# Thirteen first-layer units in seven products instead of nine, with a first product that ScalarE copies between PSUM banks, in an order given as a table

## The chip, the cores and the metric

The kernel runs on one core of one Trainium2 chip. The metric is the device time of one execution in microseconds (us). Before the change it is 273.97 us, the median of three runs (273.91 to 274.48).

## The reference

The input is q, k and v of 8 batch elements, 8 heads, 576 positions and head size 64, and four weight matrices. An attention with a window of 128 positions and a linear bias by distance feeds an MLP mixer: a token mix over the 576 positions and a channel mix of 512 to 1536 to 512 channels, each with a residual.

```python
scores = scale * np.matmul(q, k.transpose(0, 1, 3, 2))
scores = np.where(mask, scores + bias[None], -1000000000.0)     # 0 <= i - j < 128
attn = softmax(scores);  x = attn @ v                           # as (batch, 576, 512)
h = np.maximum(x.transpose(0, 2, 1) @ w_tok1, 0.0) @ w_tok2     # 576 -> 256 -> 576
u = x + h.transpose(0, 2, 1)
out = u + np.maximum(u @ w_ch1, 0.0) @ w_ch2                    # 512 -> 1536 -> 512
```

## The kernel before

The 576 positions of a batch element are four blocks of 128 and a tail of 64; the tails of two elements share a tile. Work goes in eight stages, `b` = 0 to 7, one for each element. In stage `b` TensorE (PE) does `main(b)`, the channel mix of element `b`, and between its pieces `side(b + 1)`, the attention and the token mix of the next element.

- `side`: the keys and queries of a block are turned (`qkT`, by SP's transposing DMAs from the eleventh block on), `scores` multiplies them, ScalarE (ACT) takes the exponential into `pe`, VectorE (DVE) multiplies by a mask, `values` multiplies by v, and DVE or ACT divide into `xb`. `token_mix` then does two products (`W1`, a ReLU into `r1`, `W2`); DVE adds the residual to the second one (L907) and writes `ub`, or `utl` for a tail. SP turns `ub` block by block into `uT` (L915, `utl` into `uTt`), which is the input of `main`.
- `main`, first layer: a *chunk* (L1085) is one of the twelve hidden tiles of 128: four matmuls of 128x512, and one ReLU by ACT or DVE into `r2`. A *unit* (`unit`, L1006) does four hidden tiles at once by seven products (Strassen's way) of four matmuls of 128x256 each, with sums of weights (`WS`) and of inputs (`tt`) that DVE prepares. `UNITS` says how many of the three possible units a stage has; the rest are chunks.
- `main`, second layer (`second`, L1326): always seven products, in three PSUM banks `g1`, `g2` and `g3`, with sums `s` of the hidden values. Each product is evicted by a DVE add into an output buffer (`raw` or `ob`), then stored.

PSUM has eight banks, all a tile `ps`. In a unit the banks are y, z and w. Product 1 is made in y and `keep` copies it to an output buffer e1 in SBUF (L1021 on ACT, L1022 on DVE); y goes on to take products 6, 7 and 4 on top. Product 2 is made in z, and `join` adds z and e1 on DVE into `r2` (L1030) and applies the ReLU in place (L1032 on DVE, L1034 on ACT).

The order of all instructions is made in Python while the program is built. `Plan.run` takes, for each of the five engines, the operation that can begin first by costs and ranks, chooses the buffer of each ring, and for operations with a second engine (`other`) the engine. POOL issues the loads in the order of the list `LOADS` and of the pairs after it. Each engine then runs its instructions strictly in that order and waits on semaphores. `Plan.emit` puts matmuls of zeros (L1418) into gaps that the plan sees on PE in the first 60 us, so that its clock stays up.

Of the kernel before, what the change touches and what calls it, by code (L numbers as in the profile page):

```python
# [10 lines left out]
ALU = mybir.AluOpType  # L11
# [8 lines left out]
class Buf:  # L20
    def __init__(self, ring, choice):
        self.ring, self.choice, self.slot = ring, choice, None
        self.writers, self.parts, self.users = [], {}, []
# [6 lines left out]
class Ring:  # L30
# [14 lines left out]
    def best(self, choice, skip=0):  # L45
        got = []
        for c in choice:
            ts = [self.free(i) for i in c]
            if None not in ts:
                got.append((max(ts), c))  # L50
        got.sort(key=lambda x: x[0])
        return got[skip] if len(got) > skip else None

    def take(self, b):
        b.slot = self.best(b.choice)[1]
        for i in b.slot:
            self.owner[i] = b
            self.log[i].append(b)
# [15 lines left out]
class Plan:  # L74
    def __init__(self):
        self.rings, self.ops, self.orders, self.part, self.inside = {}, [], 0, 0, {}
# [4 lines left out]
    def buf(self, name, choice=None):  # L81
        return Buf(self.rings[name], choice or self.rings[name].each)

    def op(self, eng, cost, emit, rank, makes=(), adds=(), part=None, uses=(), reads=(), needs=(),
# [8 lines left out]
        o.n = len(self.ops)  # L93
# [35 lines left out]
    def run(self):  # L129
        ops = self.ops  # L130
        for o in ops:
            o.rank += SHIFT * offset(o)
# [82 lines left out]
        while todo:  # L215
            best = None
            for e, c in cand.items():
                pick, early = None, None
                for o in c:
                    if e == "POOL" and o is not pool[sent]:  # L220
# [8 lines left out]
                    for b in o.bufs:  # L229
                        if b.slot is None:  # L230
                            got = b.ring.best(b.choice, asked.count(b.choice))
# [19 lines left out]
                if early and early[1] is not pick[1] and early[0][0] < pick[0][0] + GRACE * pick[1].cost:  # L251
# [13 lines left out]
            todo -= 1  # L265
            for b in o.bufs:
# [43 lines left out]
    def emit(self, spin):  # L310
        banks = self.rings["ps"]
        fills = []
        for a, z in self.gaps:
            if a < FILL and z - a > (250 if a > DENSE else 60):
                for i, log in enumerate(banks.log):
                    spans = [(min(u.t0 for u in b.users), max(u.done for u in b.users)) for b in log]
# [27 lines left out]
RELU = 350  # L344
SUMS_AT = 60e3
# [17 lines left out]
UNITS = [0,0,0,1,2,1,2,3]  # L363
# [22 lines left out]
def kernel(  # L386
# [51 lines left out]
    def bank(choice=ONE):  # L438
        return plan.buf("ps", choice)
# [106 lines left out]
    for i_, raw in enumerate(raws):  # L546
        buf, i = block(0, (0, RAW)[i_ // 2])["qk"], i_ % 2

        def cast(eng=dve_.tensor_copy, raw=raw, buf=buf, i=i):
# [3 lines left out]
                **({"other": ("ACT", 600, lambda cast=cast: cast(act_.copy))} if i_ > 1 else {}))  # L553
    if PADT:
        for i in range(2):
            plan.op("DVE", 190, lambda i=i: dve_.memset(W1p[(1 - i) * R : (2 - i) * R, i, :], 0.0), -90)
# [103 lines left out]
    def transposes(pr, blk, rank):  # L660
        got = held[pr, blk]["qk"]
# [35 lines left out]
    def scores(pr, blk, half, rank, behind=()):  # L697
        tail = blk == TAIL
# [5 lines left out]
        sp = [bank(TWO + THIRD + [(6, 7)])] if joint else [bank(TWO + THIRD if first else TWO) for _ in range(2)]  # L704
# [13 lines left out]
        def go():  # L718
            for i in range(4):
                for kind, kb, a, z in work:  # L720
                    for e in range(2):
                        pe_.matmul(wide(e)[:, i, 0 if joint else kind, a:z],  # L722
                                   lhsT=ts[kb]()[e * D : (e + 1) * D, NHP + i, :],
                                   rhs=ts[blk]()[e * D : (e + 1) * D, i, a:z], start=not slanted, stop=True,
                                   skip_group_check=slanted)
# [49 lines left out]
    def values(pr, blk, half, pb, rank):  # L775
        xb = xbs[pr]
# [54 lines left out]
    def token_mix(b, rank):  # L831
        pr, half = b // 2, b % 2
# [6 lines left out]
        t1 = [bank() for _ in range(NJ)]  # L839
# [12 lines left out]
        def tails():  # L852
            for j in range(NJ):
# [6 lines left out]
        plan.op("PE", 225 if xt else 432, tails, rank(216), adds=t1,  # L860
                reads=[(xb, (TAIL, k)) for k in ((0, 1) if pad and pr < HALVED else (tk,))],
                uses=[xt] if xt else [], needs=lw1 if b else lw1[:2], mode=0 if pad else 1)
# [9 lines left out]
        hts = []  # L872
        for blk in blocks:
            wide = b == 0
            if wide and blk < 2:
                hts.append(bank(TWO))
            ht = hts[blk % 2] if wide else bank()
# [3 lines left out]
            def go(blk=blk, ht=ht, hs=hs, fold=fold):  # L881
                for j in range(NJ):
# [4 lines left out]
                    else:  # L887
                        c = blk % NC
                        pe_.matmul(ht()[:, hs], lhsT=W2[:, j, c * P : (c + 1) * P], rhs=r1()[:, j, :],  # L889
                                   start=j == 0, stop=j == NJ - 1 and not fold)  # L890
# [563 lines left out]
```

## Time and profile before

| what | before |
|---|---|
| time, median of 3 runs | 273.97 us (273.91 to 274.48) |
| the profiled execution: its span, first to last instruction | 273.4 us |
| PE busy | 267.6 us, 98% of the span, 2839 matmuls |
| DVE busy | 230.4 us, 84% |
| ACT busy | 148.9 us, 54% |
| POOL busy | 112.9 us, 41% |
| granted TensorE clock, mean | 0.999 |

The profile has the span of its execution and not that execution's own device time; the median of the runs lies 0.6 us above the span, which is what lies around the instructions. Busy time counts a moment once, however many matmuls overlap in it. A matmul's recorded duration contains the way through the array, so what one costs the stream is read from the distance between starts.

### The profile page before, as it was taken

How to read it: one execution, taken by the hardware profiler on the slowest of the kernel's cores; microseconds unless marked ns; L12 is line 12 of the kernel's file. 1: busy time of each engine (PE TensorE's matmuls, PEld its weight loads, DVE VectorE, ACT ScalarE, POOL GpSimd, SP SyncE). 2: the span in 40 equal slices, each digit the busy share in tenths (PEclk: the TensorE clock that was granted, in tenths of full speed). 3: DMA queues.
4: the chain of work that ended last, by engine and by line, in shares of the span. 5: the costliest groups of instructions: out<-in, count | busy, mean ns of one | idle time of the engine just before them, and what ended most of it. 6: DMA issues, size and time to landing. Idle time of an engine off the chain costs nothing.

```text
span 273.4 us, 7106 instructions
## 1 busy us (share of the span) xinstructions
PE 267.6 (98%) x2839; PEld 190.0 (69%) x2839; DVE 230.4 (84%) x543; ACT 148.9 (54%) x258; POOL 112.9 (41%) x142
## 2 busy tenths in 40 slices
PE   8999999999999999989999999999999999999994
PEld 4675667575568556765778868586578676888884
DVE  6577799998989499855999979998898899968984
ACT  5384895356931683038951079615960596047720
POOL 8999645950770077500890007800940300040000
PEclk9999999999999999999999999999999999999999
DMA  8999999999998999999999989999996800541016
GB/s 155 154 163 174 192 199 178 153 142 236 148 146 107 179 191 119 141 166 227 116 118 155 223 172 81 139 132 210 178 155 109 217 2 0 79 134 42 1 41 192
DMA packets 167553, 38.71 MB, mean 142 GB/s; under 512 B 155872, under 2 KB 166496, under 8 KB 167520
## 3 DMA queue, kind: packets, MB, share of 16 engines
q0 software_dynamic: 113936, 19.51, 91.7%
q1 hardware_dynamic: 51360, 18.10, 36.2%
q10 hardware_dynamic: 2224, 0.66, 1.2%
q8 instruction: 22, 0.36, 0.6%
q14 instruction: 11, 0.09, 0.1%
HBM read 35.85 MB, written 9.44 MB: 166 GB/s over the span
## 4 chain that ended last, share of the span: by engine, by line
PE 94%; DMA 3%; DVE 1%; issue 0%; DVEq 0%
PE ps L1326 25%; PE ps L1085 19%; PE ps L1006 10%; PE ps L802 7%; PE ps L722 7%; PE ps L847 5%; PE ps L889 4%; PE ps L1418 4%; PE ps L1129 4%; PE ps L1218 3%; DMA uTt<-utl 3%; PE ps L679 2%; PE ps L857 1%; PE ps L885 1%; PE ps L1070 1%; PE ps L924 1%
## 5 line engine op out<-in xcount | busy, mean ns | idle before, releaser
L535 POOL DMA_DIRECT2D v<-in_v_dram x40 | 34.5, 867 | 85.8 <-PE ps L802 84.0
L757 ACT ACTIVATE pe<-ps 128x1024 bf16<-128x1024 f32 (+1 forms) x62 | 56.0, 956 | 19.7 <-PE ps L722 19.5
L1085 PE MATMUL ps<-uT,WC 128*128 128x512 bf16 x232 | 55.4, 380 | 0.0
L1326 PEld LDWEIGHTS <-r 128*128 128x128 bf16 x372 | 35.8, 98 | 6.3 <-issue 0.8
L1091 ACT ACTIVATE r<-ps 128x512 bf16<-128x512 f32 x51 | 29.9, 599 | 18.4 <-PE ps L1085 18.1
L1085 PEld LDWEIGHTS <-WC 128*128 128x128 bf16 x232 | 21.1, 97 | 20.8
L535 POOL DMA_DIRECT2D qk<-in_q_dram x38 | 33.0, 878 | 2.8 <-DMA v<-in_v_dram 2.6
L535 POOL DMA_DIRECT2D qk<-in_k_dram x38 | 33.3, 890 | 1.4 <-DMA WC<-in_moe_w_ch_dram 1.0
L767 DVE TENSOR_TENSOR pe<-pe,mask 128x1024 bf16<-128x1024 bf16 (+1 forms) x50 | 32.4, 664 | 0.9 <-ACT pe L757 0.8
L1326 PEld LDWEIGHTS <-s 128*128 128x128 bf16 x288 | 27.6, 98 | 4.8 <-issue 0.5
L818 DVE TENSOR_TENSOR xb<-ps,rt 128x256 bf16<-128x256 f32 (+1 forms) x68 | 27.3, 416 | 0.7
L802 PEld LDWEIGHTS <-pe 128*128 128x128 bf16 (+1 forms) x560 | 22.4, 98 | 6.1 <-DVE pe L767 1.2
L802 PE MATMUL ps<-v,pe 128*128 128x65 bf16 (+1 forms) x560 | 26.1, 194 | 0.0
L1326 PE MATMUL ps<-WC,r 128*128 128x256 bf16 x192 | 24.4, 273 | 0.0
L1326 PE MATMUL ps<-WT,s 128*128 128x256 bf16 x192 | 23.9, 273 | 0.0
L1326 PE MATMUL ps<-WT,r 128*128 128x256 bf16 x180 | 22.1, 273 | 0.0
L722 PEld LDWEIGHTS <-qkT 64*128 64x128 bf16 x560 | 14.8, 94 | 10.5 <-issue 8.5
L744 ACT ACTIVATE pe<-ps 128x1024 bf16<-128x1024 f32 x7 | 7.2, 1022 | 26.1 <-PE ps L722 26.1
L907 DVE TENSOR_TENSOR ub<-ps,xb 128x512 bf16<-128x512 f32 x30 | 19.0, 683 | 0.8 <-PE ps L889 0.8
L722 PE MATMUL ps<-qkT 64*128 64x128 bf16 (+1 forms) x304 | 19.3, 216 | 0.1
L815 DVE RECIPROCAL rt<-ps 128x4 f32<-128x4 f32 (+1 forms) x76 | 12.6, 176 | 6.0 <-PE ps L802 5.1
L847 PE MATMUL ps<-xb,W 128*128 128x512 bf16 x64 | 16.4, 379 | 0.0
(118 smaller groups left out, 459.4 us busy)
## 6 DMA issues: line engine op xcount, KB each, us to landing
v<-in_v_dram POOLq DMA_DIRECT2D x32, 128.0 KB, 5.3
qk<-in_k_dram POOLq DMA_DIRECT2D x30, 128.0 KB, 5.4
qk<-in_q_dram POOLq DMA_DIRECT2D x30, 128.0 KB, 5.3
WC<-in_moe_w_ch_dram POOLq DMA_DIRECT2D x8, 384.0 KB, 10.0
out_dram<-raw SPq DMA_DIRECT2D x10, 256.0 KB, 2.5
out_dram<-raw SPq DMA_DIRECT2D x18, 128.0 KB, 3.1
out_dram<-ob SPq DMA_DIRECT2D x7, 256.0 KB, 2.5
out_dram<-raw POOLq DMA_DIRECT2D x5, 256.0 KB, 2.6
```

What stands on the lines that cost most here:

```text
L535: nc.gpsimd.dma_start(out=to()[p0 : p0 + n, :, :], in_=rows(src, b, s0, n))
L722: pe_.matmul(wide(e)[:, i, 0 if joint else kind, a:z], lhsT=ts[kb]()[e * D : (e + 1) * D, NHP + i, :], rhs=ts[blk]()[e * D : (e + 1) * D, ...
L757: act_.activation(out=pb()[:, e, :, lo:, c0:c1_], in_=wide(e)[:, :, lo:, c0:c1_], func=ACT.Exp, scale=scale)
L767: dve_.tensor_tensor(out=o, in0=o, in1=heads(mk, es), op=ALU.mult)
L802: pe_.matmul(view()[a:z, at, i, :], lhsT=pb()[:, e, i, kind, a:z], rhs=vb()[:, h, 0 : D + 1], start=m == 0, stop=m == len(mms) - 1, skip_g ...
L818: dve_.tensor_tensor(out=x4(), in0=view()[r0:r1_, :, :, 0:D], in1=rt()[r0:r1_, 0:n, :, :].broadcast_to([r1_ - r0, n, 4, D]), op=ALU.mult)
L847: pe_.matmul(t1[j]()[:, :], lhsT=W1[:, c, j * P : (j + 1) * P], rhs=xb()[:, blk, :], start=c == 0, stop=False)
L907: plan.op("DVE", 690, lambda blk=blk, u=u_of(pr, blk)[1], ht=ht, hs=hs: dve_.tensor_tensor(out=u(), in0=ht()[:, hs], in1=xb()[:, blk, :], ...
L1006: pe_.matmul(bk()[:, c * HS : (c + 1) * HS], lhsT=l(c, cb), rhs=r(cb), start=new and c == 0 and cb == 0, stop=cb == 1, skip_group_check=True)
L1085: pe_.matmul(ct()[:, :], lhsT=WC1[:, cb, t * P : (t + 1) * P], rhs=uT()[:, cb, :], start=cb == 0, stop=cb == NCB - 1)
L1091: plan.op("ACT", 600, lambda t=t, ct=ct: act_.activation(out=r2()[:, t, :], in_=ct()[:, :], func=ACT.Relu), rk, part=(r2, t), uses=[ct], o ...
L1326: pe_.matmul(of(bk, c), lhsT=l(t, c), rhs=w(t), start=first, stop=g == 1 and t == HK - 1, skip_group_check=True)
```

## The change

`UNITS` goes from `[0,0,0,1,2,1,2,3]` to `[0,0,1,3,2,2,2,3]`: stage 2 gets a unit, stage 3 three instead of one, stage 5 two instead of one. Of the 96 hidden tiles of the eight stages, 52 are then made in units instead of 36.

In a unit, ACT copies product 1 from bank y to bank z (L1173 of the changed kernel), and product 2 adds on top of it in z, without the flag that starts a sum. What comes out gets its ReLU directly from PSUM. The buffer e1 and the join of z and e1 are gone. In the second layer, for all stages but the last, ACT likewise copies product 1 from g2 to g1 (L1484) and product 2 adds on top; the DVE add of product 1 into an output buffer is gone. A bank for this must be one whose last owner was written in full by matmuls (`full`, `seeded`); so that all of a bank counts as written, `scores` and the tail of `main` set the starting flag once for a bank.

The order is no longer searched while building: `ORDER` lists the operations of each engine, `SLOTS` the buffer of each, and `Plan.run` follows them. All five engines' orders differ from before, the loads on POOL too. `SEEDED` is empty, so the token mix is not seeded.

```diff
     def run(self):
         ops = self.ops
+        if SLOTS:
+            bufs = list(dict.fromkeys(b for o in ops for b in o.bufs))
+            for b, x in zip(bufs, SLOTS.split()):
+                if int(x) >= 0:
+                    b.choice = [b.choice[int(x)]]
+        lists = {e: [ops[int(x)] for x in ORDER[e].split()] for e in ORDER}
+        for e, given in lists.items():
+            for o in given:
+                if o.eng != e:
+                    o.eng, o.cost, o.emit = o.other
+                o.other = None
+        at = dict.fromkeys(lists, 0)
...
-                    if e == "POOL" and o is not pool[sent]:
+                    if lists and o is not lists[e][at[e]] or not lists and e == "POOL" and o is not pool[sent]:
                         continue
...
+ORDER = {
+    "PE": """
+        157 162 161 159 163 192 179 194 166 176 169 168 170 173 181 186 205 189 207 199 202 215 212 224 225 228 229
...
-UNITS = [0,0,0,1,2,1,2,3]
+UNITS = [0,0,1,3,2,2,2,3]
...
     def unit(b, u, rank, uT, tt, r2):
-        y, z, w = [bank(ANY if b == B - 1 or BANKS == 8 else ONE) for _ in range(3)]
-        e1, e2, e5 = [plan.buf("ob") for _ in range(3)]
+        plan.label = u
+        y, z, w = [bank(ANY if b == B - 1 or BANKS == 8 else ONE, full=True, seeded=x == 1) for x in range(3)]
+        e2, e5 = [plan.buf("ob") for _ in range(2)]
...
+        def relu(bk, rows, cols, rk):
+            mark(plan.op("ACT", 600, lambda: act_.activation(out=r2()[:, rows, cols], in_=half_of(bk), func=ACT.Relu), rk,
+                         uses=[bk], part=(r2, ("relu", rows.start, cols.start)),
+                         other=("DVE", 690, lambda: dve_.tensor_scalar(
+                             out=r2()[:, rows, cols], in0=half_of(bk), scalar1=0.0, scalar2=None, op0=ALU.max))), rows)
+
         rk = product(1, y)
-        k1 = keep(e1, y, rk)
+        k1 = plan.op("ACT", SEEDING, lambda: act_.copy(out=z()[:, :], in_=y()[:, :]), rk, makes=z, uses=[y])
         rk = product(5, w)
         k5 = keep(e5, w, rk)
-        rk = product(2, z)
-        join(e1, z, up, lo, rk)
+        rk = product(2, z, [k1], False)
+        relu(z, up, lo, rk)
         rk = product(6, y, [k1], False)
...
     def second(b, rank, r2, ss, sums, ub):
-        g1, g2, g3 = bank(SB), bank(TWO if final else SB), bank(SB)
+        g1, g2, g3 = (bank(SB, full=True, seeded=not final), bank(TWO if final else SB, full=not final),
+                      bank(SB, full=True))
...
-                            first = g == 0 and t == 0 and (c == 0 or final and bk is g2) and m not in AFTER
+                            first = (g == 0 and t == 0 and (c == 0 or final and bk is g2) and m not in AFTER
+                                     and not bk.seeded)
...
-            evict(m, bk, *DONE[m])
+            if m == 1 and g1.seeded:
+                capt[1] = plan.op("ACT", SEEDING, lambda: act_.copy(out=g1()[:, :], in_=g2()[:, :]), rank(0) - EV,
+                                  makes=g1, uses=[g2])
+            else:
+                evict(m, bk, *DONE[m])
```

Where instructions moved, on three engines. First ACT, at a stage's first unit: before, in stage 3 (`ob_111` and `raw_108` are output buffers that take products, `xb` the attention's output, `r_104` the hidden values `r2`):

```order
L757 ACTIVATE pe_85<-ps 128x1024 [waits DVE_49,PE_49]
L757 ACTIVATE pe_85<-ps 128x1024
L1021 COPY ob_111<-ps 128x512 [waits DMAHW4_49,PE_49]
L1021 COPY raw_108<-ps 128x512 [waits DMAHW3_49,DMAHW2_49,DMAHW5_49,DMAHW1_49,PE_49]
L824 ACTIVATE xb_92<-ps,rt_89 128x64 [waits DVE_49]
L824 ACTIVATE xb_92<-ps,rt_89 128x64 x3
L1034 ACTIVATE r_104<-r_104 128x2x256 [waits DVE_49]
```

And now, in stage 2, where before there was none (`r_103` is `r2` here):

```order
L1225 ACTIVATE r_103<-ps 128x512 [waits PE_49]
L875 ACTIVATE pe_87<-ps 128x1024 [waits PE_49]
L1173 COPY ps<-ps 128x512 [waits DVE_49,PE_49,Activation_49]
L875 ACTIVATE pe_87<-ps 128x1024
L1167 ACTIVATE r_103<-ps 128x2x256 [waits PE_49,Activation_49]
L1150 COPY raw_108<-ps 128x512 [waits DMAHW5_49,DMAHW2_49,DMAHW6_49,DMAHW1_49,PE_49]
```

One of the two copies into an output buffer has become the copy from bank to bank, with an exponential of 128x1024 ahead of it and one behind it; the ReLU reads PSUM instead of `r2`.

Second, SP, where it turns the `ub` of stage 4's element, before:

```order
L668 DMA_TRANSPOSE qkT_80<-qk_68 128x8x128 [waits DMASW3_49,DMAHW5_49,DMASW2_49,PE_49]
L915 DMA_TRANSPOSE uT_100<-ub_93 128x4x128 [waits DMAHW6_49,DVE_49]
L915 DMA_TRANSPOSE uT_100<-ub_93 128x4x128 [waits DMAHW7_49,DVE_49]
L915 DMA_TRANSPOSE uT_100<-ub_93 128x4x128 [waits DMAHW0_49]
L915 DMA_TRANSPOSE uT_100<-ub_93 128x4x128 [waits DMAHW1_49,DVE_49]
L1306 DMA out_dram<-raw_106 128x2x256 [waits DMAHW2_49,DVE_49]
```

And now:

```order
L782 DMA_TRANSPOSE qkT_79<-qk_70 128x8x128 [waits DMASW5_49,DMAHW3_49,DMASW4_49,PE_49]
L1044 DMA_TRANSPOSE uT_100<-ub_93 128x4x128 [waits DMAHW4_49,DVE_49]
L1044 DMA_TRANSPOSE uT_100<-ub_93 128x4x128 [waits DMAHW5_49]
L1044 DMA_TRANSPOSE uT_100<-ub_93 128x4x128 [waits DMAHW6_49,DVE_49]
L1442 DMA out_dram<-raw_107 128x2x256 [waits DMAHW7_49]
L1442 DMA out_dram<-raw_106 128x2x256 [waits DMAHW0_49]
L1044 DMA_TRANSPOSE uT_100<-ub_93 128x4x128 [waits DMAHW1_49,DVE_49]
```

The last of the four transposes now stands behind two stores.

Third, POOL, the first loads of the program, before (a number behind `qk` or `v` is a buffer, and one buffer takes both q and k of a block):

```order
L535 DMA qk_67<-in_k_dram 128x8x64
L535 DMA qk_68<-in_k_dram 64x8x64 x2
L535 DMA qk_67<-in_q_dram 128x8x64
L535 DMA qk_69<-in_k_dram 128x8x64
L535 DMA qk_69<-in_q_dram 128x8x64
L535 DMA v_72<-in_v_dram 128x8x64
L535 DMA v_73<-in_v_dram 128x8x64
```

And now:

```order
L647 DMA qk_67<-in_k_dram 128x8x64
L647 DMA qk_67<-in_q_dram 128x8x64
L647 DMA v_72<-in_v_dram 64x8x64
L647 DMA qk_68<-in_k_dram 128x8x64
L647 DMA qk_68<-in_q_dram 128x8x64
L647 DMA v_73<-in_v_dram 128x8x64
L647 DMA qk_70<-in_q_dram 64x8x64
```

The q of the first loaded block now follows its k at once, and the two small loads of tail keys come later.

108 lines of the change are left out of this document (74 added, 34 removed), and 71 rows, old and new, of tables (ORDER, SLOTS).

## The prediction

> **What bounds the kernel now.** I read the page's busy times first, then the busy time by stretch of time, then who PE waited for.
>
> ```profile
> span 273.4 us, 7106 instructions
> PE 267.6 (98%) x2839; PEld 190.0 (69%) x2839; DVE 230.4 (84%) x543; ACT 148.9 (54%) x258; POOL 112.9 (41%) x142
> ```
>
> ```profile
> core 0: us, PE busy (x) PEld busy (x) DVE busy (x) ACT busy (x) POOL busy (x), PEclk, DMA share, GB/s
> 0.00:30.00 30.00, 28.60 (x328) 18.08 (x329) 20.80 (x66) 16.74 (x30) 27.82 (x39) 1.00 1.84 164
> 30.00:110.00 80.00, 79.99 (x867) 51.10 (x865) 70.86 (x171) 48.67 (x82) 42.15 (x51) 1.00 1.66 165
> 110.00:120.00 10.00, 9.09 (x80) 6.61 (x78) 6.99 (x11) 1.26 (x2) 2.85 (x5) 1.00 1.98 133
> 120.00:145.00 25.00, 25.00 (x286) 16.85 (x284) 20.12 (x48) 17.78 (x29) 13.64 (x16) 1.00 1.48 162
> 145.00:273.40 128.40, 124.90 (x1289) 97.34 (x1286) 111.66 (x250) 64.48 (x118) 26.46 (x33) 1.00 0.85 119
> ```
>
> ```profile
> PE ps L1418 <- DVE zero L499: 1.0, 1, 1.0
> PE ps L1129 <- DMA uTt<-utl: 0.9, 1, 0.9
> PE ps L924 <- DVE ub L907: 0.3, 1, 0.3
> ```
>
> From 30 to 145 us PE rests for 0.9 us in all, at a single place: the first product on the turned tails (`uTt`). The 3.5 us missing in the last row are the end of the program, where the last eviction, store and barrier follow the last matmul. So time is PE's matmul stream and little else: PE work that goes away comes off the time in full, and every new wait in PE's order is added in full. DVE, ACT and POOL count only where they arrive late. The one stretch with something else in it is the first 30 us, where PE's busy time contains matmuls of zeros.
>
> **The units: -1.57 us.** A chunk is four matmuls of 128x512, a unit 28 of 128x256 for what four chunks do. Two rows of the chain of waits give each in a closed stream:
>
> ```profile
> 159.21 1.73 PE ps L1085 x8
> 243.44 5.26 PE ps L1006 x48
> ```
>
> 1.73 / 8 = 0.216 us for a 512-wide one, 5.26 / 48 = 0.1096 us for a 256-wide one, weight loads hidden in both. Four chunks are 16 x 0.216 = 3.46 us, a unit 28 x 0.1096 = 3.07 us. Four more units save 4 x 0.39 = 1.57 us. The order confirms the counts: 64 matmuls of 512 fewer, 112 of 256 more. All others are equal in number, and PE's changes between full and partial use of its array come 107 times in both orders.
>
> **The other engines' work: 0 while covered.** The costs are the rows of the same forms:
>
> ```profile
> L1091 ACT ACTIVATE r<-ps 128x512 bf16<-128x512 f32 x51 | 29.9, 599 | 18.4 <-PE ps L1085 18.1
> L1092 DVE TENSOR_SCALAR r<-ps 128x512 bf16<-128x512 f32 x9 | 6.2, 689 | 7.4 <-PE ps L1085 7.0 <-PE ps L1070 0.2
> L1030 DVE TENSOR_TENSOR r<-ps,raw 128x512 bf16<-128x512 f32 x18 | 12.1, 684 | 1.0 <-PE ps L1006 0.7
> L1289 DVE TENSOR_TENSOR raw<-ps,ub 128x512 f32<-128x512 f32 x20 | 13.7, 686 | 1.2 <-PE ps L1326 1.2
> L1021 ACT COPY raw<-ps x15: 566/593/672, 138.0 to 253.1; 128x512 f32<-128x512 f32 x15
> ```
>
> In the new order DVE has 25 more evictions of 0.69 us (ReLUs of chunks 9 to 19, of tails 0 to 9, of units from PSUM 1 to 4, copies 4 to 7), and loses 7 adds of the second layer and one join: about +12 us on 230. ACT gets 20 copies between banks and loses 26 chunk ReLUs: no more work than before. DVE then stands near 89% of the span. That is cover used up, not time, because PE is the fuller engine in each stretch above. Without the cover each of these evictions would be up to 0.69 us.
>
> **The copies between banks: +0.1 us.** New is that product 2 waits for product 1's copy. Behind it stands all of PE's order. The trace before has no copy into PSUM; the nearest rows are the copies into SBUF, 0.59 us. What lies between a product and its eviction shows here:
>
> ```profile
> 165.67 0.60 PE L1006 MATMUL ps<-uT,WC 128*128 128x256 bf16 x4
> 166.10 0.60 PE L1006 MATMUL ps<-tt,WS 128*128 128x256 bf16 x4
> 166.43 0.68 DVE L1030 TENSOR_TENSOR r<-ps,ob 128x512 bf16<-128x512 f32 x1
> ```
>
> The product's stream ends at 166.10, its eviction begins at 166.43: 0.33 us. With 0.59 us for the copy, product 2 may follow about 0.95 us after product 1 at the earliest. I counted the matmuls between the two in the new order, at 0.11 and 0.22 us each: of the 20 copies (13 in units, 7 in the second layer) two have 0.86 and 0.92 us, four have 1.1 us, and fourteen 1.3 us and more. Two short by about 0.05 us each give +0.1. If the copy took nothing, 0. If ACT is busy with an exponential (1.02 us, the row below) when the product ends, the six tight ones lose up to 0.9 us each: +5 us at the far end. I stay near the low end, since ACT is 46% idle.
>
> ```profile
> L757 ACT ACTIVATE pe<-ps 128x1024 bf16<-128x1024 f32 x52 | 50.6, 1023 | 17.7 <-PE ps L722 17.4
> ```
>
> The Trainium skill ("ScalarE: Activation LUTs", Step-by-step) says that ScalarE writes PSUM with less latency than SBUF; no run here shows it so far. By it the +0.1 would be 0.
>
> **The last turned blocks: +0.5 us.** PE's first product of a stage waits for the last of four `uT` transposes. What that chain takes before:
>
> ```profile
> 110.40 0.62 PE L885 MATMUL ps<-r,W2t 128*64 128x512 bf16 x4
> 110.95 1.47 PE L889 MATMUL ps<-r,W 128*128 128x512 bf16 x6
> 111.81 1.19 SPq L915 DMA_TRANSPOSE uTt<-utl  x1
> 113.10 5.83 SPq L915 DMA_TRANSPOSE uT<-ub  x4
> 118.69 1.03 PE L1129 MATMUL ps<-uTt,WC 128*128 128x256 bf16 x8 [0.92 <-DMA uTt<-utl]
> ```
>
> ```profile
> L915 SPq DMA_TRANSPOSE uT<-ub x4: 1193/1241/1717, 143.8 to 147.7; - x4
> DMA to landing us min/median/max: 4.5/5.6/6.7
> ```
>
> ```profile
> L915 SPq DMA_TRANSPOSE uTt<-utl x3: 1190/1216/1216, 111.8 to 236.0; - x3
> DMA to landing us min/median/max: 2.4/2.9/6.8
> ```
>
> The tail's product ends at 110.95, SP issues at 111.81 (0.86 us later) and PE goes on at 118.69: 7.7 us in all. In the new order 6.6 us of matmuls stand between these two, so in stage 3 the wait should be 1.1 instead of 0.92 us, +0.2. In stage 4 the old order had 15 us of matmuls between the last `W2` product and the first use of `uT`; the new one has 54 matmuls of 256 and 8 small ones, 6.1 us, with the transpose behind two stores. It needs 0.86 us to the issue and 4.5 to 6.7 us to land (the second fence: the four of stage 4 before): 5.4 to 7.6 us, a wait of 0 to 1.5 us. The middle of the landings, 5.6, gives 0.4, and I take 0.3 because the stores and loads beside it move as well. Stages 2, 6 and 7 have 3.5 to 4.4 us left for the last landing, by a count of the same kind, and the quiet landings of the third fence take 2.4 to 2.9. Low end for all this: -0.9, if stage 3's wait goes away. High end: +2.5.
>
> Two further short covers, in stage 3's token mix: the `W2` products of tail and blocks come 0.2 to 0.3 us before the ReLU of 0.69 us behind the last `W1` product can be done. +0.3.
>
> **The first 30 us: -0.5 us.** Matmuls of zeros fill PE's gaps while loads arrive. The first fence is their own busy time in that stretch, the second their last two and the first chunk:
>
> ```profile
> 0.00:30.00 30.00, 13.91 (x51) 4.72 (x51) 1.00 1.84 164
> ```
>
> ```profile
> 29.61 0.42 PE L1418 MATMUL ps<-zero 128*128 128x284 bf16 x2
> 29.87 0.38 PE L1085 MATMUL ps<-uT,WC 128*128 128x512 bf16 x1
> ```
>
> The new order has 45 in place of 51, with 20016 columns in place of 21800; the real work around them is the same until the first chunk, but for some that moved ahead. At 13.91 us for 21800 columns the difference is 1.1 us. That is what is asked for, not what data arrival grants: the q of the first loaded block comes two POOL issues earlier, `W1` four, and the last v, the block that all wait for, is the fourteenth issue as before. Bounds -1.1 and +0.5; I take -0.5.
>
> **Sum.** -1.57 + 0.1 + 0.5 + 0.3 - 0.5 = -1.2 us. The span goes from 273.4 to 272.2; with the 0.6 us around it, 273.97 becomes **272.8 us**, -0.4%. A difference under 0.2% (0.55 us) can't be told from none here.
>
> **Rivals.**
>
> 1. *All covers hold.* The matmuls alone decide, stage 3's wait halves, and the start gives up to its 1.1: 273.97 - 1.57 - 0.4 - 1.1 = 270.9 us; with the start's 0.5 it is 271.5. For it: 0.9 us of wait in 115 us of the old order. Against: the counts in stages 3 and 4. Chance 0.26; 271.5 us.
> 2. *The late transposes eat it.* Each stage from 2 to 7 ends in the same chain; landings vary from 2.4 to 6.8 us. If stages 3 and 4 wait 1.5 us more and two others 0.4 us, the sum is -1.57 + 2.3 + 0.1 - 0.5 = +0.3: 274.3 us, the same. Chance 0.12.
> 3. *Slower: ACT's queue.* The copy stands in ACT's order behind an exponential in 8 of the 20 places. If that one waits for its scores when product 1 ends, the copy begins up to 1.02 us late and PE stands still. From 0.08 us per copy on, the gain of the units is gone; at 0.2 us for each, 273.97 - 1.57 + 4.0 - 0.5 = 275.9 us. Against it: ACT is 54% busy, and products 6 waited for the same kind of copy before without a row among PE's waits. Chance 0.08.
> 4. *Weight loads bound PE.* 48 more loads in total, at 98 ns:
>
> ```profile
> L1326 PEld LDWEIGHTS <-s 128*128 128x128 bf16 x288 | 27.6, 98 | 4.8 <-issue 0.5 <-DVE s L1110 0.2
> ```
>
> If they weren't hidden, 48 x 0.098 = +4.7, less 1.57: 277.1 us. Against: 48 matmuls in 5.26 us, where a 98 ns load lies behind each 110 ns. Chance 0.02. The Trainium skill ("Perfetto Trace Analysis", Identifying the Most-Contended Engine) counts PE's room by its weight loads' busy share, 69% here, rather than by matmul busy time; by that PE would have room that the stream of starts doesn't have.
>
> That the work isn't saved at all is excluded by the counts of the order.
>
> **Chances and range.** The forecast has 0.52, with 272.1 to 273.6 as its own range. Faster by over 0.2% (under 273.42): 0.46 of it, all 0.26 of rival 1, 0.02 of rival 2: 0.74. Same: 0.06 + 0.08 = 0.14. Slower: 0.02 of rival 2, 0.08, 0.02: 0.12. The range from 271.2 to 274.2 leaves out the low tail of rival 1 and the slower cases.
>
> **What would show it.** Right: about 1.6 us less of the first-layer matmuls; 45 matmuls of zeros and the first chunk earlier than 29.87; PE waiting on `uTt` and on stage 4's `uT` among the waits; copies of 0.6 us. Wrong: PE waiting on ACT's copies in many places, matmuls of 256 at over 0.11 us, or idle time of PE over 3 us between 30 us and the last matmul.

## The result, and the profile after

The changed kernel takes **272.91 us** (median of 4 executions, 272.14 to 273.23) against 274.10 us (4, 273.91 to 274.48): a ratio of 0.995, 95% interval 0.9935 to 0.9965. Two more sets gave 0.9954 (0.9940 to 0.9969) and 0.9953 (0.9941 to 0.9965). The forecast was 272.8 us, 0.1 us off. Three terms of its sum did not come out, and one part of the difference had no term at all; the rest of this document is about those.

The weight loads of the chunks before, one for each matmul, then the page's busy line of the changed kernel and the same row of it:

```profile
L1085 PEld LDWEIGHTS <-WC 128*128 128x128 bf16 x232 | 21.1, 97 | 20.8
```

```profile
span 270.4 us, 7179 instructions
PE 264.1 (98%) x2853; PEld 194.1 (72%) x2881; DVE 240.9 (89%) x564; ACT 144.3 (53%) x264; POOL 112.7 (42%) x142
...
L1219 PEld LDWEIGHTS <-WC 128*128 128x128 bf16 x168 | 15.1, 98 | 14.7 <-issue 0.6
```

That is 64 chunk matmuls fewer, as counted; the units' weight loads went from 252 to 364 (L1006 and L1135). This trace has 2853 matmuls for 2881 weight loads: 28 records are missing, so PE's 264.1 us is some 1.7 us low (265.9 and 265.8 in the two other traces of this kernel). VectorE went up by 10.5 us to 89%, ScalarE down by 4.6, and PE is still the engine that is always busy. Who PE waited for, the whole list of that execution:

```profile
PE ps L1559 <- DVE zero L611: 1.0, 1, 1.0
PE ps L840 <- ACT qkT L799: 0.2, 1, 0.2
PE ps L1219 <- issue: 0.2, 1, 0.2
PE ps L967 <- issue: 0.2, 1, 0.2
```

The two rests of 0.2 us that name `issue` are such missing records: neither is listed in the two other traces. The wait on `uTt` is gone, none on stage 4's `uT` came, and none on a copy. Matmuls of zeros fell from 13.91 us to 12.64 in the first 30 us, and the first chunk starts earlier (columns of the first row: window, its length, PE busy, weight loads busy, granted clock, DMA share, GB/s):

```profile
0.00:30.00 30.00, 12.64 (x45) 4.17 (x45) 1.00 1.81 164
```

```profile
29.30 1.90 PE L1219 MATMUL ps<-uT,WC 128*128 128x512 bf16 x7
```

One thing does not fit: the spans of the two profiled executions differ by 3.0 us (273.4 and 270.4), the times by 1.2. That comes first.

### The profile page after: what moved, and what is told of

It reads as the page before. It is cut to its first block, busy times and chain, and to the rows that moved or that the text cites. A ratio compares the mean times of both kernels' runs of the same rounds, so it can differ in the third digit from the quotient of the medians.

```text
span 270.4 us, 7179 instructions
## 1 busy us (share of the span) xinstructions
PE 264.1 (98%) x2853; PEld 194.1 (72%) x2881; DVE 240.9 (89%) x564; ACT 144.3 (53%) x264; POOL 112.7 (42%) x142
## 4 chain that ended last, share of the span: by engine, by line
PE 92%; DVE 5%; issue 1%; DMA 1%; ACT 0%; SPq 0%; DVEq 0%
PE ps L1463 25%; PE ps L1135 15%; PE ps L1219 12%; PE ps L840 7%; PE ps L921 6%; PE ps L967 5%; PE ps L1010 4%; PE ps L1559 4%; PE ps L1353 3%; PE ps L1263 3%; PE ps L793 2%; PE ps L977 1%; DMA qkT<-qk 1%; DVE xb L937 1%; PE ps L1006 1%
## 5 line engine op out<-in xcount | busy, mean ns | idle before, releaser
L875 ACT ACTIVATE pe<-ps 128x1024 bf16<-128x1024 f32 (+1 forms) x62 | 57.4, 962 | 49.6 <-PE ps L840 49.1
L1219 PE MATMUL ps<-uT,WC 128*128 128x512 bf16 x152 | 39.7, 379 | 1.0 <-issue 0.2
L921 PEld LDWEIGHTS <-pe 128*128 128x128 bf16 (+1 forms) x560 | 23.6, 98 | 4.9 <-DVE pe L885 0.4
L937 DVE TENSOR_TENSOR xb<-ps,rt 128x256 bf16<-128x256 f32 (+1 forms) x64 | 25.6, 415 | 0.7
L1219 PEld LDWEIGHTS <-WC 128*128 128x128 bf16 x168 | 15.1, 98 | 14.7 <-issue 0.6
L1463 PE MATMUL ps<-WT,s 128*128 128x256 bf16 x192 | 25.4, 273 | 0.2
L1135 PE MATMUL ps<-tt,WS 128*128 128x256 bf16 x156 | 22.3, 273 | 0.0
L1135 PEld LDWEIGHTS <-WS 128*128 128x128 bf16 x208 | 19.1, 97 | 4.0
L1442 POOL DMA_DIRECT2D out_dram<-raw x6 | 4.3, 717 | 40.3 <-issue 37.1
L1173 ACT COPY ps<-ps 128x512 f32<-128x512 f32 x13 | 7.3, 578 | 25.7 <-PE ps L1135 14.2
```

The lines of the kernel that those rows point to most:

```text
L875: act_.activation(out=pb()[:, e, :, lo:, c0:c1_], in_=wide(e)[:, :, lo:, c0:c1_], func=ACT.Exp, scale=scale)
L921: pe_.matmul(view()[a:z, at, i, :], lhsT=pb()[:, e, i, kind, a:z], rhs=vb()[:, h, 0 : D + 1], start=m == 0, stop=m == len(mms) - 1, skip_g ...
L937: dve_.tensor_tensor(out=x4(), in0=view()[r0:r1_, :, :, 0:D], in1=rt()[r0:r1_, 0:n, :, :].broadcast_to([r1_ - r0, n, 4, D]), op=ALU.mult)
L1135: pe_.matmul(bk()[:, c * HS : (c + 1) * HS], lhsT=l(c, cb), rhs=r(cb), start=new and c == 0 and cb == 0, stop=cb == 1, skip_group_check=True)
L1219: pe_.matmul(ct()[:, :], lhsT=WC1[:, cb, t * P : (t + 1) * P], rhs=uT()[:, cb, :], start=cb == 0, stop=cb == NCB - 1)
L1463: pe_.matmul(of(bk, c), lhsT=l(t, c), rhs=w(t), start=first, stop=g == 1 and t == HK - 1, skip_group_check=True)
```

## Experiments

### What one profiled execution stands for

Four more profiled executions, two of each kernel, without an edit.

> The kernel before, unchanged, for another profiled execution of it. In the trace of before the span is 273.4 us; in the trace after it is 270.4 us with 272.14 us of time, so 1.75 us lie around the span. Theory A (what lies around the span is the same for both kernels): the profiled execution before was itself a slow one, at about 273.4 + 1.75 = 275.1 us, and another one of the same kernel has a span near 274.1 - 1.75 = 272.3 us, with the first chunk's matmul and the wait on uTt at other times than 29.87 us and 0.92 us. Theory B (0.6 us lie around the span of the kernel before): the span is 273.4 us again within 0.3 us.

> The kernel before, unchanged, for a third profiled execution. Two of them took 275.0 us and some 275.1 us, while 34 runs of it have a median of 274.0 to 274.1 us. Theory A (executions differ by how late single transposes and loads land): this one, if it is near 274 us, has its span 1 us shorter, with less of the 0.5 to 0.9 us on uTt, or an earlier first chunk than 29.87 us. Theory B (a profiled execution of this kernel is always the slow one): 275 us again.

> The changed kernel again, against the kernel before, for a narrower interval and another trace. Theory A (the forecast's sum): 1.2 us faster, a ratio of 0.9955, between 0.9945 and 0.9965. Theory B (the span's difference of 3.0 us is the real one): a ratio of 0.989.

> The changed kernel again, as the measure for the two below on the same chip, and for a third trace of it. 272.9 us, a ratio to the kernel before of 0.995 to 0.996. If single landings are what makes its executions differ, the trace differs from the two others at few places: the scores at 72 us, the scores at 120 us, or stage 7's last uT transpose, which landed 3.8 and 4.1 us after its issue in those two and 4.8 us in the trace of the kernel with two rows moved.

Measured: 275.0 us (span 273.2) and 273.92 us (span 272.2) for the kernel before; 272.96 (271.2) and 272.98 us (271.2) for the changed one, with the two ratios given above. In every execution of either kernel whose span is known, time less span is between 1.7 and 1.85 us. So the execution that the prediction was read from had taken about 275.1 us, 1.0 more than the median. The first repeat of it gave the span that theory B had named, 273.2 us, but its time of 275.0 us shows theory A's cause: 1.8 us lie around this span too, and it was a second long execution. The third, at 273.92 us, is near the median, so a profiled execution is not always the long one. It shows what the long ones had too much of:

```profile
span 272.2 us, 7106 instructions
...
PE ps L1418 <- DVE zero L499: 1.0, 1, 1.0
PE ps L924 <- DVE ub L907: 0.3, 1, 0.3
```

```profile
29.65 1.68 PE L1085 MATMUL ps<-uT,WC 128*128 128x512 bf16 x7
...
111.57 1.19 SPq L915 DMA_TRANSPOSE uTt<-utl  x1
...
117.47 1.05 PE L1129 MATMUL ps<-uTt,WC 128*128 128x256 bf16 x8
```

```profile
DMA to landing us min/median/max: 2.4/3.7/4.5
```

The turned tails landed 4.5 us after their issue at the latest (6.8 and 6.4 us in the other two), PE reached them after 5.9 us, and there was **no wait on `uTt` at all**. The only rest of PE between 30 and 145 us that the prediction found belongs to the two long executions (0.9 and 0.5 us), not to the typical one. The first chunk is also 0.2 us earlier than in the first trace; in the second one it starts at 30.10 us, and a load of weights adds a wait of 0.4 us.

The typical execution and the third trace of the changed kernel come from the same chip. PE's last group of 18 matmuls in both, and the changed kernel's start:

```profile
267.21 1.49 PE L1358 MATMUL ps<-WT,r 128*128 128x256 bf16 x18
```

```profile
28.69 0.62 PE L793 MATMUL ps<-ident,qk 128*128 128x128 bf16 x8
29.14 1.89 PE L1219 MATMUL ps<-uT,WC 128*128 128x512 bf16 x8
...
266.48 1.49 PE L1499 MATMUL ps<-WT,r 128*128 128x256 bf16 x18
```

These rows give the whole balance. Eight transposes on PE that had stood behind the first chunk now stand ahead of it (72 instead of 64 of 128 columns there by the order; the first row of the second fence shows eight of them take 29.14 - 28.69 = 0.45 us). *Start:* 29.14 - 29.65 - 0.45 = **-0.96 us**. *From the first chunk to the last group:* 267.21 - 29.65 = 237.56 us before, 266.48 - 29.14 = 237.34 us after, -0.22; the matmuls alone make -1.57 - 0.45 = -2.02, so **rests of PE grew by 1.80 us**. *Behind it:* with the spans to two places, 272.16 - 267.21 = 4.95 and 271.18 - 266.48 = 4.70, **-0.25 us**. VectorE's last eviction begins 1.5 us after this group starts and not 1.8, since five of its small memsets, 0.59 us in all, now stand behind that eviction instead of ahead of it. Together -0.96 - 1.57 + 1.80 - 0.25 = -0.98, the difference of the spans. The rests are the remainder here, so the sum cannot fail; counted the other way, as what the distances between PE's starts from 30 us on exceed those of a closed stream of the same forms, they are about 1.3 us in the typical execution before and 3.2 us in this one. By this count they grew by 1.8 to 2.0 us, depending on which distance is taken as closed. By the same subtraction the rests grew by 0.84 us in the first trace of the changed kernel (29.30, and 265.68 for the last group) and by 1.60 in the second (29.32 and 266.46).

### The copies between banks, done twice

```diff
-        k1 = plan.op("ACT", SEEDING, lambda: act_.copy(out=z()[:, :], in_=y()[:, :]), rk, makes=z, uses=[y])
+        k1 = plan.op("ACT", SEEDING, lambda: [act_.copy(out=z()[:, :], in_=y()[:, :]) for _ in range(2)], rk, makes=z, uses=[y])
```

> The changed kernel with each of the 13 units' copies between banks done twice, one behind the other on ScalarE; nothing else moves. A copy takes 0.57 us in its traces, so product 2 may follow product 1 no earlier than about 1.5 us after it in place of 0.95 us. Theory A (the copies lie on PE's path, with covers of 0.86 to about 1.5 us, as counted in the order): the shortfalls of 13 units sum to about +3 us, 275 to 277 us, and PE shows waits on ACT at the second products. Theory B (covers much longer than counted, since PE was never seen to wait for a copy): under +0.5 us, 272.8 to 273.4 us.

Measured: 278.44 us (277.95 to 279.32), 5.5 us more than the changed kernel (the changed kernel was not run beside it; the kernel before was, at 274.11 us, as against 274.10 in the first set). First the copies of the changed kernel's third trace (13 of units, 7 of the second layer), then the doubled ones with who waited for them (us, times):

```profile
L1173 ACT COPY ps<-ps x13: 570/570/620, 96.6 to 248.9; 128x512 f32<-128x512 f32 x13
...
L1484 ACT COPY ps<-ps x7: 570/570/614, 48.7 to 227.3; 128x512 f32<-128x512 f32 x7
```

```profile
L1173 ACT COPY ps<-ps x26: 570/570/617, 97.8 to 256.4; 128x512 f32<-128x512 f32 x26
...
  PE ps L1135: 3.5, 8
```

Theory A, and more than the +3 us that the covers counted in the order gave. Of 13 x 0.57 = 7.4 us added on ScalarE, 5.5 arrive in the time. The covers are uneven: eight of the second products wait, 3.5 us of idle time in all; from start to start each of these eight loses 0.50 to 0.66 us, about the length of the copy added, so they had next to no cover left. The other five lose 0.13 us at most and had 0.4 us or more. (The trace is of the longest of the four executions and has another 1.0 us of waits on a load of weights.) In the changed kernel itself PE's waits name no copy, so the term of +0.1 us measured 0. The rule that ScalarE writes PSUM sooner than SBUF (the Trainium skill, "ScalarE: Activation LUTs", Step-by-step) agrees: 0.570 us into a bank, 0.593 us into SBUF for the same tile. The 0.02 us a copy is too little to be seen in the time.

### The first loads in the old order

The changed kernel's table, POOL's list:

```diff
-        6 9 16 10 11 13 17 14 8 18 7 21 19 12 20 22 24 15 27 26 25 30 32 23 34 31 33 41 28 36 29 37 35 38 40 43 44
+        6 7 8 9 16 10 11 13 17 14 18 21 19 12 20 22 24 15 27 26 25 30 32 23 34 31 33 41 28 36 29 37 35 38 40 43 44
```

> The changed kernel with one edit in its table: the two loads of the tail's k (the second and third issue of the kernel before) stand ahead of the second block's q again, where the changed order has them later. All other orders, and the number of zeros' columns, are the changed kernel's. The first chunk's matmul stands at 29.30 and 29.32 us in two traces of the changed kernel, at 29.87 and 30.10 us in two of the kernel before, with 0.45 us more of other work ahead of it in the changed one. Theory A (the order of the first loads is what grants the earlier start): the first chunk moves back by 0.5 to 1.0 us and the time grows by as much, to 273.4 to 273.9 us. Theory B (the start is set by what is asked for, the fewer columns of zeros, or by later loads): within 0.2 us of the changed kernel.

Measured: 274.99 us (274.32 to 275.40), 1.0030 of the kernel before (1.0018 to 1.0041): 2.1 us more than the changed kernel. The edit did more than the expectation said: buffers and the matmuls of zeros follow from the order, and this kernel has 48 of these, not 45. The first chunk is at 29.80 us, 0.5 us back, as theory A has it, but the time is 1.1 us above theory A's range. Most of the other 1.6 us shows later among PE's waits, at the scores' transposes and at an eviction in the last stage:

```profile
PE ps L840 <- DMA qkT<-qk: 1.3, 2, 0.9
...
PE ps L1135 <- DVE raw L1151: 0.4, 1, 0.4
```

So the load order grants about 0.5 us at the start. That it also decides when much later transposes land is likely, since nothing else was edited, but these waits differ between executions too.

### Thirteen units in the planner's order

Once in the kernel before, once in the changed kernel without its table:

```diff
-UNITS = [0,0,0,1,2,1,2,3]
+UNITS = [0,0,0,3,3,2,2,3]
```

> The kernel before with 13 units in place of 9 and nothing else: no copies between banks, the order still the planner's. The numbers of units by stage are 0, 0, 0, 3, 3, 2, 2, 3, since the planner finds no order for the changed kernel's own numbers. Theory A (PE's matmul count decides): 1.57 us faster, a ratio of 0.994. Theory B (the covers decide: behind the four further units stand more evictions on VectorE, and the planner's order puts matmuls less than an eviction behind what they need in 66 places, 5 before): the sum of the shortfalls is over 5 us, a ratio of 1.01 to 1.03, and the new waits of PE name DVE and the values' exponentials.

> The changed kernel without its table: 13 units (0, 0, 0, 3, 3, 2, 2, 3 by stage), the copies between banks, the order the planner's. Theory A (the matmul count and VectorE's relief decide): 1.2 to 1.6 us faster than before, a ratio of 0.994 to 0.9955, as the changed kernel. Theory B (the order decides): short covers in 29 places and more columns of zeros than the table's order (22910 against 20016) cost 2 to 5 us, a ratio of 1.00 to 1.015.

Measured: **333.05 us**, a ratio of 1.216 (1.213 to 1.218), and **314.15 us**, 1.145 (1.143 to 1.147). The first kernel's main waits and two of its stretches:

```profile
PE ps L1085 <- DMA uT<-ub: 11.8, 2, 6.1
PE ps L802 <- DVE pe L767: 4.6, 4, 1.8
PE ps L1006 <- DMA uT<-ub: 4.3, 1, 4.3
PE ps L1129 <- DMA uTt<-utl: 3.9, 1, 3.9
PE ps L1006 <- DVE r L1030: 2.9, 3, 1.0
```

```profile
core 0: us, PE busy (x) PEld busy (x) DVE busy (x) ACT busy (x) POOL busy (x), PEclk, DMA share, GB/s
0.00:110.00 110.00, 108.35 (x1194) 68.32 (x1195) 91.54 (x236) 65.44 (x111) 70.24 (x90) 1.00 1.76 165
...
200.00:250.00 50.00, 38.12 (x369) 25.24 (x368) 32.46 (x68) 19.51 (x33) 15.63 (x20) 0.90 1.02 105
```

The direction is theory B's, the size some ten times what was written, and the largest waits are on turned blocks, which theory B did not name. The 1.57 us of saved matmuls vanish where too little stands between a stage's last product and the turned blocks that the next one begins with: PE rests for 4 to 6 us at a time. Since the planner's numbers belong to nine units, the two runs say nothing on an order planned anew; they say that the matmul count is worth its time only with an order that covers every chain. The second kernel is 18.9 us below the first, but its planned order is another one too, so that is not the worth of the copies alone. Nine units with the copies in an order as good as the table's were not tried.

### Loads beside the transposes

Four loads of 64 rows into unused SBUF, behind the last load that the changed kernel issues ahead of stage 3's transposes:

```diff
                 nc.gpsimd.dma_start(out=to()[p0 : p0 + n, :, :], in_=rows(src, b, s0, n))
+                if (name, pr, blk) == ("v", 2, 1):
+                    for x in extra:
+                        for r in (0, R):
+                            nc.gpsimd.dma_start(out=x[r : r + R, :, :], in_=rows(src, b, s0 + r, R))
```

> The changed kernel with four further loads of 64 rows each on POOL, behind the load of v at 109 us: as many as the kernel before had issued there, but into rows of SBUF that nobody reads. In the trace of before the turned tails landed 6.8 us after their issue at 111.8 us, with such loads in flight until about 115 us; in two traces of the changed kernel they landed after 3.8 to 4.0 us, with no load behind 109.3 us. PE uses them 5.75 us after the issue. Theory A (loads in flight beside it stretch the transpose's landing): it lands 6 to 7 us after its issue, PE waits on uTt for 0.3 to 1.3 us, and the time is 273.1 to 274 us. Theory B (the landing depends on something else, such as the transposes ahead of it): it lands within 4.5 us, no wait, 272.6 to 273.1 us.

Measured: 272.40 us (272.30 to 272.65), not slower than the changed kernel's sets (medians of 272.67 to 272.91). The transposes of stage 3 (duration on SP's queue, and the time from issue to landing), in the changed kernel and in this one:

```profile
L1044 SPq DMA_TRANSPOSE uT<-ub x4: 1199/1216/2099, 111.2 to 116.0; - x4
...
DMA to landing us min/median/max: 2.3/3.6/4.7
```

```profile
L1049 SPq DMA_TRANSPOSE uT<-ub x4: 1217/1222/1284, 111.1 to 115.1; - x4
...
  PE ps L1140: 0.2, 1
...
DMA to landing us min/median/max: 4.3/5.6/6.7
```

`uTt` landed after 5.7 us instead of 4.0. In the eight traces of this order or near it, without the added loads, it took 3.3 to 5.0 us, and the last `uT` 2.3 to 3.0 us against 4.3 here. So the landing is between what the two theories had: loads in flight do stretch a transpose, by 1 to 2 us, as theory A says, but the cover of 5.75 us that the new order has just holds, PE waits 0.2 us on one `uT`, and the time shows nothing. It bears on why the prediction's wait did not come: in the old order POOL still issued loads when SP issued the transpose of the tails (111.81 us), in the new one its last load goes out 1.2 us ahead of it (109.92 us). POOL's last issue before the transposes' end, before and after:

```profile
111.40 1.45 POOL L535 DMA_DIRECT2D qk<-in_k_dram  x2
```

```profile
108.71 0.95 POOL L647 DMA_DIRECT2D v<-in_v_dram  x1
```

The loads alone do not make the 6.8 us, for the typical execution before has the same ones and 4.5 us. In all twelve traces of either order the tails' transpose lands within 0.6 us of the last load issued before it or up to 0.4 us behind it: at 118.65 and 118.71 us in the trace that the prediction used, at 116.09 and 116.06 in the typical one, at 113.92 and 113.41 in the changed kernel. The long execution differs in that this load itself took 6.6 us to land, 4.2 in the typical one. Why it did stays open.

### The rests that are new

In stage 3's token mix PE rests for 0.36 us between two W1p products, because VectorE copies the tail rows (`xt`) behind another sum of 0.55 us. Two edits: the copy one place up, alone and together with a group of six matmuls moved up ahead of the W2 products.

```diff
-        583 668 671 669 654 655 647 651 581 649 652 587 564 662 567 665 666 568 673 590 683 588 694 688 570 820 692
+        583 668 671 669 654 655 647 651 581 649 652 587 564 662 567 665 666 673 568 590 683 588 694 688 570 820 692
```

```diff
-        667 653 818 585 650 591 555 563 661 592 664 678 679 674 675 676 680 681 677 682 597 693 687 598 691 689 600
+        667 653 818 585 650 591 555 563 661 592 664 678 679 674 675 676 680 681 677 682 600 597 693 687 598 691 689
```

> The changed kernel with two rows of its table moved, both in stage 3's token mix: on VectorE the copy of the tail rows (xt) one place up, ahead of a sum of 0.55 us, and on PE one group of six second-layer matmuls (0.66 us) up between the last W1 product and the W2 products. In two traces of the changed kernel PE rests there for 0.36 us before the second W1p pair, about 0.1 us before the tail's W2 product and 0.2 us before the next. Theory A (each rest is the queueing of that one instruction, and PE's rest is time): 0.5 to 0.7 us faster than the changed kernel, about 272.2 us, a ratio to the kernel before of 0.993 to 0.9935. Theory B (a later arrival takes its place at once: the transposes' landing or the next eviction): no difference, 272.6 to 273.1 us.

Measured with both: 273.13 us (12 executions, 272.11 to 274.64), no gain. PE's timeline, stage 3 of the changed kernel (its third trace), then of this one:

```profile
106.86 0.39 PE L977 MATMUL ps<-xb,W1p 64*128 64x512 bf16 x1
107.23 0.37 PE L977 MATMUL ps<-xt,W1p 64*128 64x512 bf16 x1
...
108.29 0.72 PE L1006 MATMUL ps<-r,W2t 128*64 128x512 bf16 x4
...
120.75 0.23 PE L840 MATMUL ps<-qkT 64*128 64x128 bf16 x2 [0.49 <-DMA qkT<-qk]
```

```profile
107.23 0.39 PE L977 MATMUL ps<-xb,W1p 64*128 64x512 bf16 x1
107.24 0.39 PE L977 MATMUL ps<-xt,W1p 64*128 64x512 bf16 x1
...
108.97 0.62 PE L1006 MATMUL ps<-r,W2t 128*64 128x512 bf16 x4
...
121.41 0.23 PE L840 MATMUL ps<-qkT 64*128 64x128 bf16 x2 [0.89 <-DMA qkT<-qk]
```

The rest of 0.36 us is gone, and 0.89 us stands at 121 us. The scores there wait for a transpose of `qk` that SP issues behind the five of `u`, and these follow the W2 products, which stand 0.68 us later here: the group of six puts them 0.66 us back, the copy brings them 0.36 us forward, and 0.37 us come from earlier in this execution (0.3 us of it at the scores at 72 us). It took 274.01 us, 0.9 more than the median of its kernel, so its 0.89 us need not be typical. In the copy-alone version the W2 products come forward instead:

> The changed kernel with one row of its table moved: on VectorE the copy of the tail rows (xt) one place up, ahead of a sum of 0.55 us, in stage 3. In the kernel with this and PE's group moved, the matmuls up to the turned tails gained, but the W2 products stood behind 0.66 us more of work, so the blocks were turned later and PE waited 0.8 us more for the scores' transposes at 121 us. Theory A (the wait moved because the chain of products, transposes and scores was put back, not because a rest must come back): with the copy alone the rest of 0.36 us before the second W1p pair goes, the W2 products and the transposes come 0.3 us earlier, and the time falls by 0.2 to 0.4 us against the changed kernel in the same runs. Theory B (whatever is gained ahead of the transposes is waited for behind them): no difference within 0.2 us.

Measured: 272.04 us (6 executions, 271.31 to 273.32), a ratio of 0.9937 (0.9914 to 0.9960), against 272.67 us (272.33 to 272.98) of the changed kernel beside it. The two W1p products stand at 106.74 us together, the tail's W2 product at 107.82, 0.47 us earlier (0.14 of it from the start), and no wait is listed at the scores. So theory A in the trace; the means differ by 0.52 us with a standard error of 0.34, which does not settle it for the time.

The last stage has a second new rest. VectorE's first sum of turned blocks (`tt`) waits for stage 7's last transpose with two evictions queued behind it. All that follows on VectorE is late, and 5.7 us later PE waits for one of its copies. The changed kernel's third trace, VectorE and then PE:

```profile
243.53 0.42 DVE L1099 TENSOR_TENSOR tt<-uT 128x512 bf16<-128x512 bf16 x1 [2.04 <-DMA uT<-ub]
243.87 1.28 DVE L1271 TENSOR_SCALAR r2t<-ps 128x512 bf16<-128x512 f32 x2
```

```profile
249.19 0.60 PE L1135 MATMUL ps<-tt,WS 128*128 128x256 bf16 x4 [0.34 <-DVE raw L1151]
```

```diff
-        1269 1399 1273 1277 1354 1377 1423 1355 1401 1426 1356 1281 1357 1381 1385 1361 1370 1390 1367 1427 1387
+        1269 1399 1273 1277 1401 1377 1354 1423 1355 1426 1356 1281 1357 1381 1385 1361 1370 1390 1367 1427 1387
```

> As the kernel with the copy alone, and besides in the last stage on VectorE two evictions of the tails' first-layer products (0.68 us each) ahead of the first sum of turned blocks (tt), which waits for stage 7's last uT transpose. In the traces where this transpose lands after 4.7 to 5.0 us, VectorE sits idle for 2.5 us with these evictions queued behind the waiting sum, and PE loses 0.3 us at once and 0.6 us at an eviction later; in those with 3.8 to 4.1 us PE loses nothing. Theory A (the loss is VectorE's queue behind the late landing): a narrower spread, no execution with the 0.6 us, on average 0.2 to 0.5 us faster than the kernel with the copy alone. Theory B (the landing itself is what PE waits for): no difference to it within 0.2 us.

Measured: 272.28 us (5 executions, 271.78 to 272.68), a ratio to the kernel before of 0.9937 (0.9924 to 0.9950). VectorE now:

```profile
240.75 0.69 DVE L1271 TENSOR_SCALAR r2t<-ps 128x512 bf16<-128x512 f32 x1
241.63 0.69 DVE L1271 TENSOR_SCALAR r2t<-ps 128x512 bf16<-128x512 f32 x1 [0.18 <-PE ps L1263]
243.17 0.42 DVE L1099 TENSOR_TENSOR tt<-uT 128x512 bf16<-128x512 bf16 x1 [0.85 <-DMA uT<-ub]
```

The transpose landed 4.7 us after its issue, later than the 4.2 us in the trace of the changed kernel shown above, yet PE has no wait on `L1151`. The spread is 0.9 us against the copy-alone version's 2.0, its mean the same (272.24 and 272.17). Theory A in the mechanism, while the 0.2 to 0.5 us on average were not shown. Against the changed kernel in the same runs the mean is 0.45 us lower, with a standard error of 0.21: probably the better version of all, by about as much as can be told.

## Why the prediction was right, and where it was not

*The base.* "The span goes from 273.4 to 272.2; with the 0.6 us around it" was wrong twice, in ways that cancel: 1.75 us lie around a span, and 273.4 was the span of a 275.1 us execution. It goes from 272.2 to 271.2. The 0.6 was a subtraction of two different executions. PE's rests were undercounted too. Between 30 us and the last group, busy time leaves out 0.01 us in the typical execution before and 1.0 us in the changed kernel's third trace, the distances between starts about 1.3 and 3.2 us, because a recorded 0.38 us of a matmul covers a slot of 0.216 us. By the second count the third trace is past the prediction's own sign of being wrong, 3 us.

*Units, -1.57 us:* right. 168 chunk matmuls with 64 fewer by the order, and 256-wide ones still 0.11 us apart (four groups of four, 0.44 us from start to start, in the timelines). 512-wide ones stay at 0.216. No run measured the term alone; the two ways of counting PE's rests above agree within 0.2 us, and the saved matmuls enter only one of them.

*VectorE's 12 us, 0 while covered:* 10.5 us more, 89% as said. It was not entirely covered: the 0.36 us at `xt` and the 0.34 us at the last stage's eviction are VectorE's queue.

*Copies, +0.1 us:* close in size, no wait being listed, though eight of the thirteen covers in units are nearly used up, thinner than the count in the order said.

*Turned blocks, +0.5 us:* wrong. The step carried the chain's 7.7 us from one order to another, landing included. The landing was 6.8 us in a long execution whose loads landed late; it was 4.5 us in the typical one, and 3.5 to 4.0 us in three traces of the new order, with 5.75 us of cover. In stage 4 the cover of 6.1 us came as counted, but the chain took 5.0: with two stores ahead of it the transpose was issued 2.4 us after the last product instead of 0.86, and then landed after 2.6 us instead of 4.5 to 6.7. The term should have been 0, or -0.9 against that execution. The same transposes cost time elsewhere: at the scores behind them in SP's queue (0 to 0.49 us at 121 us) and at the last stage's sum. That is rival 2's mechanism at places it did not name.

*Token mix, +0.3 us:* the place was right, the mechanism for the smaller part: a rest of 0.1 us names the ReLU ahead of the tail's `W2` product, and 0.36 us the copy of the tail rows.

*The three together, +0.9 us:* 0.84, 1.60 and 1.80 us in three traces. From start to start, 0.36, 0.56 and 0.50 us of the last are the three places above (`xt`, the scores at 121 us, the last stage's eviction); some 0.4 us are smaller rests, which the list of waits leaves out and whose causes are open.

*First 30 us, -0.5 us:* too careful; -0.96 us, near the bound of -1.1 that the columns of zeros gave. The shorter time behind the last group, -0.25 us, had no term.

So that 272.8 us came out within 0.1 us is luck: a start that was 0.5 us better and an end 0.25 us better paid for 0.9 us more of rests in the third trace. The way down, fewer matmuls and an earlier start against some new rests, was as forecast. Rival 1's 271.5 us was missed by these rests. Rivals 3 and 4 did not occur: no wait on a copy is listed, and PE's weight loads, 194 us, hid as before.

## What to carry to other kernels

Before arguing about single microseconds, set the profiled execution's time against the median, and take a second profile: a wait on a transfer that stands in one trace may not be in the typical one. When an order changes, carry over what a chain issues, not how long its transfers took, since a landing depends on which loads fly beside it. An instruction that waits for a transfer on an engine that works in order should have nothing behind it that is ready, and a rest is to be mended by bringing its producer forward, not by filling it with work that puts a later chain back.

## What the runs showed of the hardware

*The granted clock falls with PE's rests.* In the thirteen-unit kernel in the planner's order, PE was 98% busy up to 110 us at a granted clock of 1.00, then 76% busy from 200 to 250 us at 0.90, and a matmul of 128x512 there took 503 ns on average in place of 380:

```profile
L1085 PE MATMUL ps<-uT,WC 128*128 128x512 bf16 x16 | 5.5, 503 | 5.7 <-DMA uT<-ub 5.7
```

Right behind the longest rest of that stretch the clock is 0.50 (third column from the end of the second row):

```profile
215.41 3.57 PE L1085 MATMUL ps<-uT,WC 128*128 128x512 bf16 x8 [5.66 <-DMA uT<-ub]
```

```profile
215.80:219.00 3.20, 3.20 (x11) 0.96 (x11) 1.18 (x3) 0.60 (x1) 0.00 (x0) 0.50 1.13 160
```

The eight matmuls take 0.44 us each from start to start in place of 0.216, some 1.8 us more together. So a rest of 5.7 us cost more than itself here, and part of the 59 us that this kernel lost is clock. The Trainium skill ("TensorE: Matmul & The Clock Gate", Part 1: The HAM clock gate) says that the default is half rate and sustained activity releases it; the stretch agrees: 0.50 after the rest, and 1.00 again from 219.3 us on, when matmuls had followed each other for 4 us.

*A transpose's landing goes with the loads beside it.* The same four transposes took 3.6 us in the middle without the four added loads of 64 rows and 5.6 us with them, one trace each; and in twelve traces the tails' transpose landed within 0.6 us of a load issued around it.
